# Issuing the stores of h and the attention transposes at group heads instead of at score bursts

## The chip, the cores and the metric

The kernel runs on one core of one Trainium2 chip. The metric is the device time of one execution in microseconds (us). Where the text says "shift", it compares two traces: how much earlier the same instruction starts, with the difference of the kernels' starts (up to 0.4 us, in one run 1.27 us) taken off, measured at the first residual add of the stage. Each trace is of one execution.

## The reference, cut to what matters

```python
def _A_ref(x, wqkv, wo):                 # 32 heads of 32, window of 256
    qkv = ...(x @ wqkv)...
    p = softmax(where(mask, q @ k.T * Dh ** -0.5, -1e9))
    return (p @ v) @ wo
def _B_ref(x, w1, w2):
    return silu(x @ w1) @ w2

h  = x + _A_ref(_layernorm(x), wqkv, wo)      # x: 2048 x 1024 bf16
h2 = h + _B_ref(_layernorm(h), w1, w2)        # w1: 1024 x 3584
```

## The kernel before

The work goes in four blocks of 512 rows. While TensorE (PE) does the dense matmuls of one block, it does the attention of another in bursts between them (a burst is a short row of score matmuls). The last such stage is 24 dense groups of the output projection (blocks 0 to 2) with the attention of block 3 in between. Each pair of groups completes one tile of 128 rows of h, which is stored to memory. Block 0 of h is read back within the same stage (`L497`), normalised, and transposed by DMA (`L203`) for the MLP that follows. VectorE (DVE) adds the residual to each half tile and does the norms. All these DMAs are issued by one sequencer, SP, in program order.

Two kinds of DMA are not issued where their data is made, but put on the list `late`: the store of a finished tile of h (`L276`) and the transpose of a head group's attention output (`L413`). `run_late` issues what is on the list.

```python
def run_late():
    while late:
        late.pop(0)()

def wo_group(b, j, c, between=None):
    acc = next_acc()                                   # one of two PSUM banks
    for g in range(G):
        if between: between(g)
        nc.tensor.matmul(acc, lhsT=qT[b][...], rhs=wo[...], ...)              # L271
    nc.vector.tensor_tensor(out=t_out[j % 2][...], in0=acc,
                            in1=r_in[(b * 4 + j) % 6][...], op=ALU.add)       # L273
    if c == 1:
        late.append(lambda: nc.sync.dma_start(out=h_dram[...], in_=t_out[j % 2]))  # L276

class Stream:                                          # ... cut
    def between(self, kt):
        if self.seen * 20 >= self.done * 192:
            run_late()                                 # at each burst of scores
            self.bursts[self.done]()
            self.done += 1
        ...                                            # cut: attention outputs

# the last stage; the stage of the dense groups before it is built alike
for n in range(24):
    if n % 2 == 0 and n >= 2 and n // 2 + 5 < S // P:
        load_res(n // 2 + 5)                           # residual load, L258
    wo_group(*dense[n], stream.between)
    if n in (1, 4, 7, 12, 15):
        load_w1((1, 4, 7, 12, 15).index(n))            # L518
    if n == 9:
        steps = ln2_steps(0); steps.pop(0)()           # reads block 0 of h, L497
    if n == 17:
        nc.sync.dma_start(out=w2[0], in_=w2_v[:, 0:4, :])                     # L595
    ...                                                # cut: steps of the layer norm
```

The softmax here doesn't subtract the row's maximum and nothing guards it: scores larger than these inputs give would overflow.

Of the kernel before, what the change touches and what calls it, by code (L numbers as in the profile page):

```python
# [48 lines left out]
def kernel(  # L49
# [89 lines left out]
    def load_x(b, j, queue=nc.sync):  # L139
        queue.dma_start(out=x_ring[(b % 2) * 4 + j], in_=x2d[(b * 4 + j) * P:(b * 4 + j + 1) * P, :])  # L140
# [94 lines left out]
    def v_group(b, j, c, copy, between=None):  # L235
        acc = next_acc()
        for kt in range(KT):
            if between:
                between(kt)
            nc.tensor.matmul(acc, lhsT=lnT_b[b % 2][:, kt, j * P:(j + 1) * P], rhs=wv[:, kt, c * 512:(c + 1) * 512],  # L240
                             start=(kt == 0), stop=(kt == KT - 1))
        copy(out=v[:, b * 4 + j, c * 16:(c + 1) * 16, 0:DH], in_=acc.rearrange("p (h d) -> p h d", d=DH))

    def qk_group(b, which, g, copy, between=None):
        acc = next_acc()
        col0 = which * D + g * P
        for kt in range(KT):
            if between:
                between(kt)
            nc.tensor.matmul(acc, lhsT=wqk[:, kt, col0:col0 + P], rhs=lnT_b[b % 2][:, kt, :],  # L250
                             start=(kt == 0), stop=(kt == KT - 1))
        copy(out=(qT, kT)[which][b][:, g, :], in_=acc)  # L252
# [4 lines left out]
    def load_res(t):  # L257
        nc.sync.dma_start(out=r_in[t % 6], in_=x2d[t * P:(t + 1) * P, :])  # L258
# [3 lines left out]
# [5 lines that stand above are left out]
        acc = next_acc()  # L267
        for g in range(G):
            if between:
                between(g)  # L270
            nc.tensor.matmul(acc, lhsT=qT[b][:, g, j * P:(j + 1) * P], rhs=wo[:, g, c * 512:(c + 1) * 512],  # L271
                             start=(g == 0), stop=(g == G - 1))
        nc.vector.tensor_tensor(out=t_out[j % 2][:, c * 512:(c + 1) * 512], in0=acc,  # L273
                                in1=r_in[(b * 4 + j) % 6][:, c * 512:(c + 1) * 512], op=ALU.add)
        if c == 1:
            late.append(lambda: nc.sync.dma_start(out=h_dram[(b * 4 + j) * P:(b * 4 + j + 1) * P, :], in_=t_out[j % 2]))  # L276
# [139 lines left out]
    def attn_piece(b, g, first, last):  # L416

        for k in range(2):
            a, z = max(first - 16 * k, 0), min(last - 16 * k, 16)
            if a < z:  # L420
                attn_out(b, g + k, a, z)
                if z == 16:
                    late.append(lambda k=k: attn_transpose(b, g + k))

    class Stream:
# [7 lines left out]

        def between(self, kt):
            if self.seen * 20 >= self.done * 192:
                run_late()
                self.bursts[self.done]()
                self.done += 1
            if self.seen * 40 >= (self.given * 2 + 1) * 192:
                if pending:  # L440
                    pending.pop(0)()
                coming.append(lambda b=self.b, n=self.given: attn_piece(b, n // 5 * 2, *SPLIT[n % 5]))
                if len(coming) > 2:
                    pending.append(coming.pop(0))
                self.given += 1
            self.seen += 1
# [38 lines left out]
    def ln1_steps(b):  # L485
        st, rs = ln_tiles("a")
        xs = [x_ring[(b % 2) * 4 + j] for j in range(4)]
        steps = [lambda j=j: ln_stats(xs[j], st, j) for j in range(4)]
        steps += rstd_steps(st, rs)
        for j in range(4):  # L490
            steps.append(lambda j=j: ln_norm(xs[j], st, rs, j))
        return steps, [lambda j=j: ln_transpose(xs[j], lnT_b[b % 2], j) for j in range(4)]

    def ln2_steps(b):
        st, rs = ln_tiles("b")
        hb = h_blk[b]
        load = lambda: nc.sync.dma_start(out=hb, in_=h_dram[b * 512:(b + 1) * 512, :].rearrange("(j p) d -> p j d", p=P))  # L497
        steps = [load]
        steps += [lambda j=j: ln_stats(hb[:, j, :], st, j) for j in range(4)]
        steps += rstd_steps(st, rs)  # L500
        for j in range(4):
            steps.append(lambda j=j: ln_norm(hb[:, j, :], st, rs, j))
        turns = [lambda j=j: ln_transpose(hb[:, j, :], ln2T[b], j) for j in range(4)]
        return steps[:-2] + [turns[0], steps[-2], turns[1], steps[-1]] + turns[2:]
# [12 lines left out]
    def load_w1(kt):  # L517
        nc.sync.dma_start(out=w1[:, kt, :], in_=w1_v[:, kt, :])  # L518
# [32 lines left out]
    for b in range(2, NB):  # L551
        stream = Stream(b - 1)
        dense = [lambda j=j, c=c: v_group(b, j, c, dve, stream.between) for j in range(4) for c in range(2)]
        dense += [lambda w=w, g=g: qk_group(b, w, g, dve, stream.between) for g in range(G) for w in range(2)]
        if b + 1 < NB:
            for j in range(4):
                load_x(b + 1, j)
            steps, turns = ln1_steps(b + 1)
        else:
            steps, turns = [], []  # L560
            nc.sync.dma_start(out=wo[:, 0:4, :], in_=wo_v[:, 0:4, :])
            nc.sync.dma_start(out=wo[:, 4:8, :], in_=wo_v[:, 4:8, :])
            load_res(0)
            load_res(1)
        for n in range(24):
            if b == NB - 1 and n in (4, 10, 14):
                load_w1({4: 7, 10: 6, 14: 5}[n])
            dense[n]()
            if steps and n >= 1 and n != 3:
                steps.pop(0)()  # L570
            elif turns and n % 3 == 2:
                turns.pop(0)()
        assert not steps and not turns
# [9 lines left out]
    steps = []  # L583
    stream = Stream(NB - 1)
    for n in range(24):
        if n % 2 == 0 and n >= 2 and n // 2 + 5 < S // P:
            load_res(n // 2 + 5)
        wo_group(*dense[n], stream.between)
# [3 lines that stand above are left out]
            steps = ln2_steps(0)  # L592
            steps.pop(0)()
        if n == 17:
            nc.sync.dma_start(out=w2[0], in_=w2_v[:, 0:4, :])  # L595
        for _ in range(1 if n < 16 else 2):
            if steps and n >= 12:
                steps.pop(0)()
# [105 lines left out]
```

## Time and profile before

| | before |
|---|---|
| time, first three runs | 696.37, 696.53, 699.1 us |
| span of the profiled run | 695.9 us |
| PE busy | 687.7 us |
| idle PE at tile 6's wait, at tile 10's wait, before the MLP | 0.39, 0.59, 1.97 us |
| read of block 0 of h (`L497`) issued | 254.16 us |
| last transpose of the MLP's input (`L203`) landed | 290.61 us |

A tile's number counts the tiles of 128 rows of h; tile t is made by groups 2t and 2t + 1. "Landed" is the time at which the DMA's completion semaphore is full, in the trace.

### The profile page before, as it was taken

What the parts mean: (1) busy time and instruction counts of PE and PEld (TensorE: products, weight loads), DVE (VectorE), ACT (ScalarE), POOL (GpSimd) and SP (SyncE); (2) the same over time, 40 slices, a digit from 0 to 9 for tenths busy, and PEclk for the clock granted to TensorE, in tenths of its full rate; (3) what the DMA queues carried; (4) which work ended last, traced back from release to release, by engine and by line L of the source; (5) the groups of instructions that cost most, each with busy time, mean ns of one, the idle gap of its engine ahead of it and who ended that gap; (6) DMA issues with size and microseconds to landing.
All of it is one profiled execution on the core that took longest, in us unless ns stands there. A gap on an engine that the chain in (4) does not pass through costs nothing.

```text
span 695.9 us, 13820 instructions
## 1 busy us (share of the span) xinstructions
PE 687.7 (99%) x5859; PEld 330.0 (47%) x5859; DVE 292.0 (42%) x616; ACT 240.7 (35%) x400; POOL 161.6 (23%) x295
## 2 busy tenths in 40 slices
PE   8999999999999999899999999999999999999998
PEld 3444455555555555444444444444444444444445
DVE  6267646744444438544315134433133251244111
ACT  4326656666666666421310023300033100233000
POOL 1007666666666656500000000000000000000000
PEclk9999999999999999999999999999999999999999
DMA  7732241236462988970023410023200023100110
GB/s 241 257 59 72 33 103 43 25 64 179 74 131 19 237 238 247 231 285 31 31 75 99 106 38 1 1 89 71 83 1 1 11 95 91 45 1 1 30 39 24
DMA packets 76462, 60.93 MB, mean 88 GB/s; under 512 B 50288, under 2 KB 60528, under 8 KB 76400
## 3 DMA queue, kind: packets, MB, share of 16 engines
q1 hardware_dynamic: 76256, 59.78, 32.7%
q8 instruction: 46, 0.75, 0.5%
q10 hardware_dynamic: 144, 0.26, 0.1%
q14 instruction: 16, 0.13, 0.1%
HBM read 39.85 MB, written 8.39 MB: 69 GB/s over the span
## 4 chain that ended last, share of the span: by engine, by line
PE 94%; DVE 2%; DMA 1%; issue 1%; POOL 1%; SPq 0%; ACT 0%; DVEq 0%; POOLq 0%
PE hacc L614 19%; PE hacc L651 17%; PE acc L250 16%; PE acc L651 10%; PE acc L614 9%; PE acc L240 8%; PE acc L271 4%; PE o_ps L377 3%; PE sc L302 2%; PE hacc L271 1%; PE o_ps L392 1%; DVE ln_st L171 1%; DMA h_dram<-r_t 1%; PE sc L348 1%; DVE r_t L273 1%
## 5 line engine op out<-in xcount | busy, mean ns | idle before, releaser
L368 POOL TENSOR_SCALAR_AFFINE_SELECT r_e<-r_e 128x512 bf16<-128x512 bf16 (+1 forms) x288 | 158.6, 568 | 127.6 <-ACT r_e L357 64.9
L651 PEld LDWEIGHTS <-r_a 128*128 128x128 bf16 x952 | 90.9, 98 | 103.0
L614 PEld LDWEIGHTS <-r_w 128*128 128x128 bf16 x896 | 87.4, 98 | 107.2 <-issue 2.4
L651 PE MATMUL hacc<-r_a 128*128 128x512 bf16 (+2 forms) x616 | 122.5, 360 | 0.0
L614 PE MATMUL hacc<-r_e,r_w 128*128 128x512 bf16 x456 | 100.9, 379 | 0.0
L314 ACT ACTIVATE r_e<-sc 128x768 bf16<-128x768 f32 x96 | 78.2, 814 | 49.9 <-PE sc L302 49.9
L623 ACT ACTIVATE r_n<-hacc 128x512 f32<-128x512 f32 x30 | 17.9, 597 | 178.9 <-PE hacc L614 178.9
L651 PE MATMUL acc<-r_a 128*128 128x512 bf16 x336 | 74.0, 379 | 0.0
L250 PEld LDWEIGHTS <-r_w 128*128 128x128 bf16 x512 | 44.9, 97 | 47.3 <-issue 0.2
L252 DVE CAST r_a<-acc 128x512 bf16<-128x512 f32 x56 | 38.6, 690 | 57.1 <-PE acc L250 57.1
L250 PE MATMUL acc<-r_t,r_w 128*128 128x512 bf16 x256 | 61.7, 379 | 0.0
L250 PE MATMUL acc<-r_w 128*128 128x512 bf16 x256 | 59.9, 379 | 0.0
L271 PE MATMUL acc<-r_o,r_a 128*128 128x512 bf16 x208 | 52.4, 379 | 1.1 <-DVE r_t L273 1.0
L614 PE MATMUL acc<-r_e,r_w 128*128 128x512 bf16 x216 | 49.1, 379 | 0.0
L377 PEld LDWEIGHTS <-r_e 128*128 128x128 bf16 x1152 | 37.8, 96 | 14.2
L357 ACT ACTIVATE r_e<-sc 128x1024 bf16<-128x1024 f32 x36 | 34.9, 1021 | 21.2 <-PE sc L348 20.1
L377 PE MATMUL o_ps<-r_a,r_e 128*128 128x33 bf16 x1152 | 38.3, 178 | 0.0
L666 DVE SCALAR_TENSOR_TENSOR r_t<-hacc,r_t 128x512 bf16<-128x512 f32 (+2 forms) x22 | 14.0, 635 | 57.0 <-PE hacc L651 57.0
L315 ACT ACTIVATE r_e<-sc 128x256 bf16<-128x256 f32 x96 | 37.6, 392 | 0.0
L666 DVE SCALAR_TENSOR_TENSOR r_t<-acc,r_t 128x512 bf16<-128x512 f32 x12 | 8.3, 691 | 64.2 <-PE acc L651 64.2
L624 DVE SCALAR_TENSOR_TENSOR r_a<-r_n,hacc 128x512 bf16<-128x512 f32 x30 | 20.6, 687 | 33.1 <-ACT r_n L623 33.1
L271 PEld LDWEIGHTS <-r_a 128*128 128x128 bf16 x256 | 21.8, 97 | 24.0 <-issue 2.1
(75 smaller groups left out, 539.5 us busy)
## 6 DMA issues: line engine op xcount, KB each, us to landing
r_w<-in_B_w_dram SPq DMA_DIRECT2D x8, 896.0 KB, 7.1
r_a<-in_B_w_dram SPq DMA_DIRECT2D x7, 1024.0 KB, 7.8
r_w<-in_A_wqkv_dram SPq DMA_DIRECT2D x6, 1024.0 KB, 8.7
h_dram<-r_t SPq DMA_DIRECT2D x16, 256.0 KB, 3.2
r_t<-h_dram SPq DMA_DIRECT2D x16, 256.0 KB, 2.8
out_dram<-r_t SPq DMA_DIRECT2D x31, 128.0 KB, 1.7
r_o<-in_A_x_dram SPq DMA_DIRECT2D x15, 256.0 KB, 3.9
r_e<-h_dram SPq DMA_DIRECT2D x3, 1024.0 KB, 5.6
```

What stands on the lines that cost most here:

```text
L240: nc.tensor.matmul(acc, lhsT=lnT_b[b % 2][:, kt, j * P:(j + 1) * P], rhs=wv[:, kt, c * 512:(c + 1) * 512], start=(kt == 0), stop=(kt == KT ...
L250: nc.tensor.matmul(acc, lhsT=wqk[:, kt, col0:col0 + P], rhs=lnT_b[b % 2][:, kt, :], start=(kt == 0), stop=(kt == KT - 1))
L252: copy(out=(qT, kT)[which][b][:, g, :], in_=acc)
L271: nc.tensor.matmul(acc, lhsT=qT[b][:, g, j * P:(j + 1) * P], rhs=wo[:, g, c * 512:(c + 1) * 512], start=(g == 0), stop=(g == G - 1))
L314: nc.scalar.activation(out=tri[:, :, :, 64:256], in_=both, func=ACT.Exp, scale=scale)
L315: nc.scalar.activation(out=e[:, 1024:1280].rearrange("p (h q) -> p h q", q=P), in_=bank[:, :, 192:320], func=ACT.Exp, scale=scale)
L357: nc.scalar.activation(out=e, in_=sc[pair], func=ACT.Exp, scale=scale)
L368: nc.gpsimd.affine_select(out=dst, in_=src, pattern=[[0, n] for n in dst.shape[1:-1]] + [[sgn, P]], compare_op=ALU.is_ge if upper else ALU ...
L377: nc.tensor.matmul(o_ps[pair][:, qt * 2 + hh, 0:VW], lhsT=chunk_of(i, bank, piece, pair, hh), rhs=v[:, b * 4 + kt, g * 4 + pair * 2 + hh, ...
L614: nc.tensor.matmul(acc, lhsT=w1[:, kt, ft * P:(ft + 1) * P], rhs=ln2T[b][:, kt, :], start=(kt == 0), stop=(kt == KT - 1))
L651: nc.tensor.matmul(acc[:, 0:c1 - c0], lhsT=gT[:, ft, j * P:(j + 1) * P], rhs=w2[ft // 4][:, ft % 4, c0:c1], start=(ft == 0), stop=(ft == F ...
L666: nc.vector.scalar_tensor_tensor(out=t_out[j % 2][:, c0:c1], in0=acc[:, 0:c1 - c0], scalar=0.5, in1=t_in[j % 2][:, c0:c1], op0=ALU.mult, o ...
```

## The change

The intent: issue the stores and the transposes at the head of each dense group, and not in the middle of one.

```diff
         def between(self, kt):
             if self.seen * 20 >= self.done * 192:
-                run_late()
                 self.bursts[self.done]()
                 self.done += 1
@@
         for n in range(24):
+            run_late()
             if b == NB - 1 and n in (4, 10, 14):
                 load_w1({4: 7, 10: 6, 14: 5}[n])
             dense[n]()
@@
     stream = Stream(NB - 1)
     for n in range(24):
+        run_late()
         if n % 2 == 0 and n >= 2 and n // 2 + 5 < S // P:
             load_res(n // 2 + 5)
         wo_group(*dense[n], stream.between)
```

## The prediction

> **What bounds the kernel now.** I began with the page: busy times, then the chain that ended last, then TensorE's (PE's) idle time.
>
> ```profile
> PE 687.7 (99%) x5859; PEld 330.0 (47%) x5859; DVE 292.0 (42%) x616; ACT 240.7 (35%) x400; POOL 161.6 (23%) x295
> PE 94%; DVE 2%; DMA 1%; issue 1%; POOL 1%; SPq 0%; ACT 0%; DVEq 0%; POOLq 0%
> ```
>
> PE is busy 687.7 of 695.9 us, so all its idle time is 8.2 us, and no reordering of transfers can give more: 8.2/695.9 = 1.2%, below 2%. Where is that idle time? The change touches the attention output transposes and the stores of h, so I tabulated engines by stretch over the output-projection stage, 227 to 291 us: the 24 groups of L271, the stores of L276, the residual loads of L258. Columns: stretch, length, busy PE, PEld, DVE, ACT, POOL, then PE clock, DMA share, GB/s.
>
> ```profile
> 227.00:254.00 27.00, 27.00 (x463) 14.28 (x454) 11.59 (x25) 18.33 (x32) 17.54 (x29) 1.00 0.93 231
> 254.00:289.00 35.00, 33.73 (x570) 17.75 (x569) 23.88 (x60) 22.46 (x40) 23.16 (x37) 1.00 0.94 242
> 289.00:291.00 2.00, 0.19 (x1) 0.13 (x2) 0.57 (x1) 0.00 (x0) 0.81 (x2) 1.00 0.95 257
> ```
>
> PE is full until 254, then loses 35.00 - 33.73 = 1.27 us, then 1.81 us: 3.08 us in all. In the stretch before 254 nothing can be won. The timeline of PE (start, length, what, and in brackets the idle time before) says where it is lost:
>
> ```profile
> 262.63 1.02 PE L271 MATMUL acc<-r_o,r_a 128*128 128x512 bf16 x4 [0.39 <-DVE r_t L273]
> 283.57 0.59 PE L271 MATMUL acc<-r_o,r_a 128*128 128x512 bf16 x2 [0.59 <-DVE r_t L273]
> 290.81 1.45 PE L614 MATMUL acc<-r_a,r_w 128*128 128x512 bf16 x6 [1.97 <-issue]
> ```
>
> The first two wait for a residual add (L273) that frees one of two accumulators. The third is the first matmul of the MLP. And the timeline of DVE for the adds that came late:
>
> ```profile
> 261.89 0.69 DVE L273 TENSOR_TENSOR r_t<-acc,r_a 128x512 bf16<-128x512 f32 x1 [4.11 <-PE o_ps L377]
> 277.31 0.69 DVE L273 TENSOR_TENSOR r_t<-acc,r_t 128x512 bf16<-128x512 f32 x1 [0.95 <-DMA h_dram<-r_t]
> 282.82 0.69 DVE L273 TENSOR_TENSOR r_t<-acc,r_a 128x512 bf16<-128x512 f32 x1 [1.98 <-PE sc L302]
> ```
>
> These are the first halves of row tiles 6, 9 and 10, with 2 output buffers: each must wait for the store of the tile two before. That store's issue and time to landing: tile 4, 255.14 + 6.7 = 261.8; tile 7, 271.50 + 5.7 = 277.2; tile 8, 277.00 + 5.7 = 282.7. All three agree with the adds' starts within 0.1 us, so the releaser named in the first and third lines is not the true one; it is the store. The SP queue around the end of the stage:
>
> ```profile
> 269.17 1.20 SPq L413 DMA_TRANSPOSE r_a<-r_n  x1
> 270.41 0.58 SPq L518 DMA_DIRECT2D r_w<-in_B_w_dram  x1
> 271.08 0.38 SPq L258 DMA_DIRECT2D r_a<-in_A_x_dram  x1
> 271.50 0.43 SPq L276 DMA_DIRECT2D h_dram<-r_t  x1
> 272.03 0.58 SPq L595 DMA_DIRECT2D r_a<-in_B_w_dram  x1
> ...
> 284.85 1.53 SPq L413 DMA_TRANSPOSE r_a<-r_n  x1
> 286.42 2.66 SPq L203 DMA_TRANSPOSE r_a<-r_a  x2
> 289.18 0.53 SPq L276 DMA_DIRECT2D h_dram<-r_t  x1
> ```
>
> L203 are the transposes of the MLP's first input. The last two sit behind an attention transpose (L413) that was held until DVE's norm at 284.78; they land 2.8 us after issue, the last one about 290.6, and PE starts at 290.8. The page calls this wait "issue"; the first weight load of the MLP waits in the program on the four L203, so I read it as the last of these.
>
> **What the Trainium skill says.** (1) "Perfetto Trace Analysis", section "DMA Instruction — HWDGE (DVE, Sync)": the reported window is only the sequencer's issue, the data movement is not in it, and the completing semaphore write comes after the write is confirmed, which can take surprisingly long when the target is HBM. The trace agrees: tile 4's store has an issue of 0.42 us and lands after 6.7 us. (2) "DMA: Bandwidth & Descriptors", section "Anatomy of one DMA": DMA engines do not wait on semaphores, the wait sits on the issuing sequencer. So one blocked entry holds all behind it on that queue. The trace agrees: SP issued nothing between 282.82 and 284.85 although the two L203 behind L413 were to come. (3) Same page, "Queues, rings and completion order": each DMA engine takes descriptors in ring order. The trace agrees in so far as small stores issued behind 1 MB loads land after 5.7 us, against 2.4 us at 289.18.
>
> **The change part by part.** I compared the two built programs' instruction order. PE, DVE, ACT and POOL: the same instructions in the same order, nothing added or removed (only some semaphore numbers differ). On SP the first 70 entries of 185 are identical, so everything before about 233 us, with three attention blocks' worth of transposes, does not change at all, although the diff touches that loop too. Entries 70 to 109 are permuted, all within the output-projection stage:
> - Each h store now stands ahead of the next residual load. Both wait for the same add, so the store goes out one load issue earlier: 0.33 to 0.43 us by the SP timeline, and ahead of 256 KB of data. The load goes later by the same, but is used ten groups later: free.
> - L413 is issued at a group head. It follows the 1 MB read of h (L497), where it went before it. Its results are read only in the MLP stage, and its source has three buffers: free, except for what stands behind it.
> - The w1 load that stood behind the L413 of 269.17 now stands before it. Its group ended near 267, so I expect it 3 to 4 us earlier. The DMA share was 0.18 in 268:269 and 0.00 in 269:270, so this fills a hole of some 2 us, and the store of tile 7 no longer queues behind that load's start.
> - The last two L203 now stand before the L413. The first is ready at once, at about 282.9; the second waits for its norm, which ended at 284.21. Issued at about 284.3, with 2.8 to 3.7 us to land, it is there at 287.1 to 288.0. PE's last group of the stage ends at 288.84.
>
> Sum on the path: the gap before the MLP falls from 1.97 to about 0: 1.97. The stall by tile 8's store: that store goes out about 1 us sooner (behind L413, ahead of a load) and has less in front; the 0.59 goes. A smaller slowness at 274.41 (five matmuls take 1.53 us and not 1.24, 0.29) belongs to the late add chain, and I count half, 0.15. Tile 6's stall of 0.39 stays: tile 4's store still stands behind L497, now with an L413 (1.20 us of issue) between, while L497 itself may go 0.4 to 0.7 us sooner, because tile 3's store does. I put 0.3 us of loss there. Sum: 1.97 + 0.59 + 0.15 - 0.3 = 2.4 us. 696.5 - 2.4 = 694.1 us, or 0.35%.
>
> **The rivals.**
> (a) *Nothing moves*: the DMA share is 0.94 in 254:289, so the same bytes might land at the same time in whatever order, and the MLP still starts at 290.8. For it: landing times of 5 to 6 us show a backlog. Against it: the share in 286:288 is 0.45 and 0.58, so the last two transposes waited for issue, not for the engines. Time then: 696.5.
> (b) *A new head-of-queue wait*: L413 now stands behind L497, which waits for tile 3's store, and it in turn holds tile 4's store. If it costs that store 1.5 us, tile 6's add and PE slip as much, the layer-norm work behind moves too, and with the other gains kept the sum is about -0.9: 695.6. If L413's own norm comes late near 276, it delays tile 8's store as well: up to 697.
> (c) *More than I count*: tile 6's stall goes too, and all 3.08 us of the stage: 693.4. Past that lie only idle stretches that the change does not reach.
>
> **Range and chances.** The most it can win is about 3.1 us (693.4); (a) and (b) reach 697. The three runs of before spread from 696.37 to 699.1, so I widen a little: 692.8 to 697.0. A gain over 2% would be 13.9 us, more than PE's whole idle time, so faster has 0.01. A loss over 2% would need 14 us of new stalls from 40 permuted entries: 0.01. Within 2%: 0.98.
>
> **What would show it right or wrong.** In the changed profile: PE busy still 687 to 688; all up to 230 us the same within 0.1; in the SP timeline the last two L203 before the L413, issued by about 285.7; the idle before the first L614 matmul under 0.4 us and its start at 288 to 289; the w1 load at 266 to 268 and the DMA hole at 269 filled; the 1.98 us DVE wait for tile 10 under 1; the one for tile 6 still 3.5 to 5. I am wrong if the first L614 matmul starts at 290 or later: then transfers, not their order, set it; or if a stall at tile 5 to 7 eats the gain.

## The result, and the profile after

The changed kernel takes 693.59 us (median of 4 runs, 693.36 to 693.7) against 697.74 us for the kernel before (4 runs, 696.37 to 699.1). The ratio is 0.994, 95% interval 0.9914 to 0.9966. A ratio is the mean time of one kernel's runs over the mean of the other's of the same rounds, so it is not quite the ratio of the medians quoted beside it. By the 2% rule this is "same", as predicted, but it is clear of noise. The span in the trace fell by 4.0 us, from 695.9 to 691.9.

In the changed kernel, lines from the removed one to the first added one are numbered one less, and lines behind the second one more: `L496` is the read of h, `L517` the w1 load, `L615` the first MLP matmul.

The page of the changed kernel, engines and chain:

```profile
PE 687.3 (99%) x5859; PEld 330.1 (48%) x5859; DVE 292.5 (42%) x616; ACT 240.8 (35%) x400; POOL 161.8 (23%) x295
PE 99%; DMA 0%; DVE 0%; issue 0%
```

PE has the same work. The chain that ends last is now PE for 99%, where 5% of it had been DVE, DMA, issue and POOL. The same three stretches as in the prediction:

```profile
227.00:254.00 27.00, 27.00 (x463) 14.29 (x459) 11.54 (x25) 18.33 (x32) 17.61 (x29) 1.00 0.96 245
254.00:289.00 35.00, 35.00 (x589) 18.88 (x590) 24.82 (x60) 22.55 (x41) 23.60 (x38) 1.00 1.05 252
289.00:291.00 2.00, 2.00 (x26) 1.05 (x23) 0.69 (x1) 0.51 (x1) 0.00 (x0) 1.00 0.76 167
```

All the idle time of PE in this stage is gone. DVE's timeline for the three adds that were late (first halves of tiles 6, 9 and 10):

```profile
259.58 0.69 DVE L273 TENSOR_TENSOR r_t<-acc,r_a 128x512 bf16<-128x512 f32 x1 [1.85 <-PE acc L271]
...
274.81 0.69 DVE L273 TENSOR_TENSOR r_t<-acc,r_t 128x512 bf16<-128x512 f32 x1
...
279.49 0.69 DVE L273 TENSOR_TENSOR r_t<-acc,r_a 128x512 bf16<-128x512 f32 x1 [0.82 <-PE acc L271]
```

They start 2.31, 2.50 and 3.33 us earlier than before. Where DVE still waits (the two brackets), it is for PE's own result. And PE's timeline where the stage ends:

```profile
286.12 1.02 PE L271 MATMUL acc<-r_o,r_a 128*128 128x512 bf16 x4
286.98 1.89 PE L615 MATMUL acc<-r_a,r_w 128*128 128x512 bf16 x8
```

The first MLP matmul starts at 286.98, not 290.81, and no bracket stands behind it: no wait. I laid the matmuls of the two traces side by side in order (5859 in each). The changed kernel is ahead by 0.05 us up to tile 6's wait, then gains 0.55 us at 262.6, 0.29 at 275.4, 0.81 at 283.6 and 2.13 at the MLP's start: 3.78 us in four steps. From there to the end nothing changes.

Why is this more than the idle time that the PE timeline shows (0.39 + 0.59 + 1.97)? A matmul of 512 columns stands in the trace with 0.379 us, but in an unbroken row one starts every 0.216 us (eight take 1.89 us in all: (1.89 - 0.379)/7). Records overlap, so each break in the row shows about 0.16 us less idle time than it costs: 0.39 + 0.16 = 0.55, 1.97 + 0.16 = 2.13; at 283.6 this rule gives 0.75, and the rest of the 0.81 was gained at 278. The 0.29 has no bracket in the timeline, but PE is busy 1.87 of the 2.00 us from 274 to 276: 0.13 us idle, and 0.13 + 0.16 = 0.29. The Trainium skill warns of this in kind ("Perfetto Trace Analysis", section "Tensor Engine Instruction (MATMUL, LD_WEIGHTS)"): a matmul's end is computed from its size and not observed.

The queue of SP in the changed kernel, in two places (with the read of h, and with the last transposes):

```profile
248.00 0.33 SPq L276 DMA_DIRECT2D h_dram<-r_t  x1
248.37 0.43 SPq L258 DMA_DIRECT2D r_t<-in_A_x_dram  x1
250.62 0.38 SPq L496 DMA_DIRECT2D r_a<-h_dram  x1
251.11 2.28 SPq L413 DMA_TRANSPOSE r_a<-r_n  x1
253.49 0.53 SPq L276 DMA_DIRECT2D h_dram<-r_t  x1
...
275.98 1.64 SPq L203 DMA_TRANSPOSE r_a<-r_a  x1
278.14 0.33 SPq L276 DMA_DIRECT2D h_dram<-r_t  x1
278.52 0.43 SPq L258 DMA_DIRECT2D r_t<-in_A_x_dram  x1
279.01 5.49 SPq L203 DMA_TRANSPOSE r_a<-r_a  x3
284.60 1.21 SPq L413 DMA_TRANSPOSE r_a<-r_n  x1
```

The last three transposes of the MLP's input go out in one row, and the attention transpose behind them. The last lands at 286.58, 0.40 us ahead of its use. In all ten traces that show a wait before the MLP, PE starts 0.20 us after the last of these landings, whatever releaser the trace names; so it is this landing that ends the wait, and 0.2 us of room are left here. The surprise is the read of h: issued at 250.62, not at 254.16. The queue of the kernel before, for that place:

```profile
248.04 0.33 SPq L258 DMA_DIRECT2D r_t<-in_A_x_dram  x1
248.42 0.43 SPq L276 DMA_DIRECT2D h_dram<-r_t  x1
250.72 1.20 SPq L413 DMA_TRANSPOSE r_a<-r_n  x1
254.16 0.38 SPq L497 DMA_DIRECT2D r_a<-h_dram  x1
254.63 0.46 SPq L258 DMA_DIRECT2D r_a<-in_A_x_dram  x1
255.14 0.42 SPq L276 DMA_DIRECT2D h_dram<-r_t  x1
```

The read of h has to wait until tile 3 is stored. Before, that store landed at 254.09; now at 250.57, although it was issued only 0.42 us earlier. While SP waited, it issued nothing else, and the DMA engines ran dry. Engines by stretch for 252 to 256 us, before and then after (the last two columns are the DMA share and GB/s):

```profile
252.00:256.00 4.00, 4.00 (x83) 2.43 (x82) 1.98 (x4) 2.84 (x7) 3.12 (x6) 1.00 0.59 59
```

```profile
252.00:256.00 4.00, 4.00 (x85) 2.44 (x84) 1.94 (x4) 2.84 (x7) 3.13 (x6) 1.00 1.00 278
```

### The profile page after: what moved, and what is told of

It reads as the page before. It is cut to its first block, busy times and chain, and to the rows that moved or that the text cites. A ratio compares the mean times of both kernels' runs of the same rounds, so it can differ in the third digit from the quotient of the medians.

```text
span 691.9 us, 13823 instructions
## 1 busy us (share of the span) xinstructions
PE 687.3 (99%) x5859; PEld 330.1 (48%) x5859; DVE 292.5 (42%) x616; ACT 240.8 (35%) x400; POOL 161.8 (23%) x295
## 4 chain that ended last, share of the span: by engine, by line
PE 99%; DMA 0%; DVE 0%; issue 0%
PE hacc L615 19%; PE hacc L652 17%; PE acc L250 16%; PE acc L652 10%; PE acc L615 9%; PE acc L240 8%; PE acc L271 7%; PE o_ps L377 4%; PE sc L302 3%; PE hacc L271 1%; PE o_ps L392 1%; PE sc L348 1%; PE sc L328 1%; DMA r_o<-in_A_x_dram 0%; PE tp L218 0%; DVE ln_st L171 0%
## 5 line engine op out<-in xcount | busy, mean ns | idle before, releaser
L652 PEld LDWEIGHTS <-r_a 128*128 128x128 bf16 x952 | 90.9, 98 | 103.0
L615 PEld LDWEIGHTS <-r_w 128*128 128x128 bf16 x896 | 87.5, 98 | 105.0
L615 PE MATMUL hacc<-r_e,r_w 128*128 128x512 bf16 x456 | 100.9, 379 | 0.0
L615 PE MATMUL acc<-r_e,r_w 128*128 128x512 bf16 x216 | 49.1, 379 | 0.0
L615 PE MATMUL hacc<-r_a,r_w 128*128 128x512 bf16 x144 | 32.9, 379 | 0.0
```

The lines of the kernel that those rows point to most:

```text
L615: nc.tensor.matmul(acc, lhsT=w1[:, kt, ft * P:(ft + 1) * P], rhs=ln2T[b][:, kt, :], start=(kt == 0), stop=(kt == KT - 1))
L652: nc.tensor.matmul(acc[:, 0:c1 - c0], lhsT=gT[:, ft, j * P:(j + 1) * P], rhs=w2[ft // 4][:, ft % 4, c0:c1], start=(ft == 0), stop=(ft == F ...
```

## The experiments

Twelve runs were made, two of them of the kernels before and after again; all gave correct results. The questions: is it the order on the queue or the amount of data that sets each landing; which half of the change does it; and are the named effects all there is?

**1. The last two transposes alone.** The kernel before; in group 21 nothing is flushed at the bursts, but at the head of group 22.

```diff
-                run_late()
+                if not hold[0]:            # hold[0] is set for n == 21
+                    run_late()
@@ last stage, head of the loop
+        if n == 22:
+            run_late()
```

> The kernel before with one reordering alone: in group 21 of the last attention stage nothing is flushed at the bursts, so the last two transposes of the MLP's input (L203) go ahead of the attention transpose that they stood behind. Theory A (order: PE waited 1.97 us at the MLP's start because these two were issued late): they are issued about 2 us sooner, the idle time before the first L614 matmul falls from 1.97 to between 0 and 0.8 us, the stalls of 0.39 and 0.59 us before it stay, and the kernel gains 1.3 to 2.1 us. Theory B (throughput: the DMA engines are busy anyway and data lands when it lands): the idle time stays at 1.5 us or more and the gain is under 0.5 us.

Measured: 695.67 us against 697.65 (ratio 0.9964, 0.9943 to 0.9985). PE's timeline in this run (its lines are renumbered: `L272` is the projection's matmul, `L620` the MLP's):

```profile
262.33 1.02 PE L272 MATMUL acc<-r_o,r_a 128*128 128x512 bf16 x4 [0.32 <-DVE r_t L274]
283.11 0.59 PE L272 MATMUL acc<-r_o,r_a 128*128 128x512 bf16 x2 [0.48 <-DVE r_t L274]
288.83 1.89 PE L620 MATMUL acc<-r_a,r_w 128*128 128x512 bf16 x8 [0.44 <-issue]
```

The earlier stalls stay, the wait before the MLP falls from 1.97 to 0.44 us, and the MLP starts 1.75 us earlier. Theory A is right for this part, in the presence of the other stalls. The last transpose was issued 3.1 us sooner (284.44 against 287.77, with 0.23 us of that the start), but landed only 1.8 us sooner (288.62 against 290.61, less the same 0.23). So it took 4.2 us from issue to landing and not 2.8, and a part of what the order gives is lost there.

**2 and 3. The two halves.** Run 2 takes the kernel before and issues only the stores at the group heads. Run 3 takes the changed kernel and issues only the transposes there, while the stores stay at the bursts. Both split the list by kind.

```diff
 # run 2                                        # run 3
 between:  run_late(("turn",))                  run_late(("store",))
 head:     run_late(("store",))                 run_late(("turn",))
```

> Half of the change: the stores of h are issued at the head of a group, ahead of the residual load, but the attention transposes at the bursts as before. Theory A: the stalls of L271 (0.39 and 0.59 us of idle PE, 1.65 us of shift together with the slow spot at 275) are the stores' doing and vanish or more than halve, gain 1.0 to 1.7 us; the MLP's start still waits, 1 to 2 us, because the last two L203 still stand behind the held attention transpose. Theory B: the stalls stay within 0.3 us of what they were. Theory C (the transposes of the attention output ahead of the w1 loads and the h read are what delays the stores): as B for the stalls, and the gain comes in the twin run instead.

> The other half: attention transposes are issued at the head of a group and the stores of h at the bursts, behind the residual load, as before. Theory A: the MLP's start no longer waits (idle under 0.5 us, gain about 2 us), while the stalls of L271 at tiles 6, 9 and 10 stay for the most part (0.5 to 1.6 us of shift). Theory C: the stalls vanish here too and the gain is that of the whole change, 3.8 us in the trace. Theory B: no more than 0.5 us gained.

Measured: run 2 took 694.78 us (ratio 0.9961, 0.9941 to 0.9981), run 3 694.49 us (0.9963, 0.9935 to 0.999; one of its six runs took 699.27, at a granted clock of 0.995). In run 2 the stalls of the stage vanish and the MLP still waits, 1.26 us, as theory A has it. In run 3 the MLP does not wait, but theory A missed the rest: 0.55 and 0.81 us were gained at tiles 6 and 10 as well, though every store stands behind the residual load. The MLP starts 3.48 us earlier with the transposes alone, 2.36 with the stores alone, 3.78 with both. The halves overlap. Theory C is out too: it wanted the stalls to stay in run 2. What both have in common with the whole change is an early read of h: 251.86 and 251.56 us.

**4. The changed kernel with the attention transpose held in front of the last two again.**

```diff
         def between(self, kt):
             if self.seen * 20 >= self.done * 192:
+                if hold[0]:                # hold[0] is set for n == 21
+                    run_late()
                 self.bursts[self.done]()
```

> The changed kernel with one step undone: in group 21 the attention transpose is flushed at the burst again, so the last two L203 stand behind it and behind DVE's norm. Theory A: the MLP's start waits again, 1 to 2.1 us of idle PE before the first L614 matmul, the rest of the gain (1.7 us) stays, so the kernel is 1 to 2.1 us slower than the changed one. Theory B: under 0.4 us slower, as in the changed kernel the last L203 lands only 0.4 us ahead of need and the engines are busy.

Measured: 694.54 us (ratio 0.9952, 0.9931 to 0.9973). PE's timeline:

```profile
289.60 1.89 PE L620 MATMUL acc<-r_a,r_w 128*128 128x512 bf16 x8 [2.03 <-issue]
```

In this trace the wait is back in full, and the gains at tiles 6 to 10 stay (1.65 us of shift): 2.19 us of shift undone (3.78 - 1.59). But it was taken of the slowest of six executions: it took 696.23 us, the other five 694.06 to 694.76. By the clock, the changed kernel run later on took 693.93 us, so 0.6 us less and not the 1 to 2.1 us expected; the two were not in the same rounds. Together with run 1 this shows that the place of this one transpose brings a wait before the MLP; how much it costs in most executions is not shown.

**5. The waits for stores taken away by another means.** The kernel before with its order, but three output buffers for the tiles.

```diff
+    t_out3 = [*t_out, view(r_a, 32768, 1024)]
@@ wo_group
-        nc.vector.tensor_tensor(out=t_out[j % 2][...], in0=acc,
+        to = t_out[j % 2] if b == NB - 1 else t_out3[(b * 4 + j) % 3]
+        nc.vector.tensor_tensor(out=to[...], in0=acc,
                                                # cut: the store, which reads to
```

> The kernel before with the queue's order untouched, but three output buffers of h for the twelve tiles of the stage and not two, so that no residual add has to wait for the store of two tiles before. Theory A1 (PE's stalls at 262.6, 275.4 and 283.6 us are the adds' wait for a store and nothing else): these stalls vanish, 1.65 us by the trace, and the wait at the MLP's start stays, 1.5 to 2.2 us of idle PE. Rival A2 (the adds are late for another reason, DVE's own load or the residual's load): under 0.5 us of shift before the MLP.

Measured: 695.39 us against 697.89 (ratio 0.9973, 0.9954 to 0.9993). The shift before the MLP is 1.65 us, the number expected to the hundredth: A1 is shown. The releasers that the trace named for two of these waits (PE) were wrong, as the prediction read them. The wait before the MLP fell to 1.17 us, lower than expected: DVE, no longer held up, had the norms ready sooner, and the held transpose went out at 281.73.

**6. What tile 3's store queued behind.** The kernel before with one w1 load moved from before that store to behind it.

```diff
-        if n in (1, 4, 7, 12, 15):
-            load_w1((1, 4, 7, 12, 15).index(n))
+        if n in (1, 4, 8, 12, 15):
+            load_w1((1, 4, 8, 12, 15).index(n))
```

> The kernel before with one load moved: the 896 KB of w1 that is issued after group 7, in front of the store of tile 3, is issued after group 8, behind that store. It tests why tile 3's store landed at 254.1 us before and at 250.6 to 251.7 in three reordered versions. Theory W (the store queues behind this load, whose last piece comes late): the store lands within 3.5 us of its issue at 248.4, so by 252, and the read of h is issued by 252.3 and not at 254.2. Rival X (the w1 load has no part in it; the time is the store's own): the store still lands 5 us or more after its issue. For the time of the kernel I expect within 1 us of before, as the load then stands in front of the read of h.

Measured: 697.0 us (ratio 0.9987, 0.9966 to 1.0009). The queue of SP:

```profile
248.66 0.43 SPq L276 DMA_DIRECT2D h_dram<-r_t  x1
249.14 0.42 SPq L518 DMA_DIRECT2D r_w<-in_B_w_dram  x1
...
252.34 0.46 SPq L497 DMA_DIRECT2D r_a<-h_dram  x1
```

The store landed at 251.70, 3.04 us after issue and not 5.67, and the read of h was issued at 252.34. Theory W holds: in the kernel before, the store waited behind the w1 load. It does not say why the store lands sooner in the changed kernel, where this load still stands in front (244.94); no run isolates that. In the trace tile 6's stall is gone, the wait before the MLP stays (1.91 us), and the MLP starts 1.16 us earlier than before. The clock shows no gain. One reason is in the trace, which is of the slowest of four executions (698.12 us, mean granted clock 0.997): right behind the wait, the granted clock (the column before the DMA share) halves.

```profile
290.00:293.50 3.50, 3.50 (x22) 1.47 (x21) 0.00 (x0) 0.18 (x1) 0.00 (x0) 0.51 0.74 182
```

The MLP's first eight matmuls take 3.40 us here and not 1.89. The traces of the kernel before, of run 4 and of run 11 have waits of 1.97 to 2.03 us there and a clock of 1.00 behind them, so that the wait brings it about is not shown.

**7. Both effects by other means.** Run 5's third buffer and run 1's order of the last two, nothing else.

> Neither half of the change as such, but both of its effects by other means: three output buffers, and the last two transposes of the MLP's input ahead of the attention transpose (as in the first experiment). If the account is full (1.65 us of waits for stores and 1.75 to 2.1 us at the MLP's start), no PE stall is left in the stage (all under 0.3 us), the first L614 matmul starts 3.3 to 3.9 us earlier than before, and the time is that of the changed kernel within 0.6 us. If the change did something else besides, this kernel stays 1 us or more behind it.

Measured: 694.7 us (ratio 0.9955, 0.9939 to 0.9972). A miss: by the clock it stays 0.77 us behind the changed kernel of the same rounds (run 8), where at most 0.6 was expected, and in the trace:

```profile
288.13 1.89 PE L622 MATMUL acc<-r_a,r_w 128*128 128x512 bf16 x8 [1.18 <-DVE r_a L276]
```

The stage's stalls are gone, but PE waits 1.18 us before the MLP although the last three transposes now go out in one row. The last lands at 287.93, and PE starts 0.20 us later; DVE, named as releaser, had ended its add before that transpose landed (last add 286.99 + 0.69 = 287.68). The shift is 2.44 us, 1.34 short of the changed kernel. So the order of those last two matters (runs 1 and 4) but is not enough.

**8. The changed kernel again.**

> The changed kernel again, on the same chip as the three others, for the comparison and for a second trace: no PE stall over 0.1 us between 227 and 291 us, the last transpose of the MLP's input landing before 287.3, time 3.3 to 4.6 us under before.

Measured: 693.93 us (693.73 to 694.03) against 697.89 (ratio 0.9943, 0.9928 to 0.9958). The shift is 3.78 us once more, the last transpose landed at 286.66. This trace lacks 111 matmul records, and shows eight gaps of 0.16 us between groups for it; no other idle time in the stage.

**9 and 10. Is it the last w1 load?** In the changed kernel it is issued at 263.92 and not at 270.41, ahead of the stretch from 268 to 270 us in which the DMA engines had been nearly idle (shares 0.18 and 0.00). Run 9 undoes that (the flush at the bursts of group 15), run 10 adds it to run 7.

```diff
 # run 9, on the changed kernel; run 10, on run 7
-        hold[0] = n == 21                      -        hold[0] = n == 21
+        hold[0] = n == 15                      +        hold[0] = n in (15, 21)
```

> The changed kernel with another step undone: after group 15 the attention transpose is flushed at the burst, so the last w1 load (896 KB) stands behind it again, and behind DVE's norm that it waits for. The run with both other effects left 1.18 us of idle PE at the MLP's start. Theory W (the last load, 4 us earlier, fills an idle stretch of the DMA engines near 269 us, and the last transposes land earlier for it): that load is issued at about 267.5 and not at 263.9, the last L203 lands near 288.1 and not 286.6, PE waits 0.8 to 1.4 us at the MLP's start, and no other stall returns; 0.8 to 1.4 us slower than the changed kernel. Rival V (the place of the load does not matter; the two other effects were short of the whole for some other reason, such as where the stores stand): idle under 0.3 us and the time of the changed kernel.

> The run with both effects by other means, and as a third the last w1 load ahead of the attention transpose after group 15. Theory W: now the account is full: the last L203 lands by 287.0, the idle time at the MLP's start falls from 1.18 to under 0.3 us, the first L614 matmul starts 3.5 to 4.0 us earlier than before (corrected for the start), and the time is that of the changed kernel within 0.6 us. Rival V: 1 us or more of idle time stays.

Measured: run 9 took 694.0 us (ratio 0.9946, 0.9933 to 0.9959), with the load at 268.44, no wait before the MLP and a shift of 3.75 us. Theory W falls: in the changed kernel the load's place is worth nothing. Run 10 took 694.23 us (0.9948, 0.9934 to 0.9962), and its trace still has 0.64 us of idle PE before the MLP, with a shift of 2.97 us. That lies between the two theories (under 0.3, 1 or more). The trace is of its slowest execution (695.74 us, the other four 693.69 to 694.35), with a start late by 1.27 us, so I don't lean on the 0.53 us of shift that it has over run 7.

**11. The kernel before again.**

> The kernel before, for a second trace. If its stalls are of the program and not of one execution: idle PE of 0.3 to 0.6 us near 262.6 and near 283.6 and of 1.7 to 2.2 us before the first L614 matmul, within 0.3 us of those times.

Measured: 697.82 us (ratio 1.0002, 0.998 to 1.0023). The waits at 283.2 (0.76 us) and before the MLP (2.02 us) are there. The one at tile 6 has no bracket, but its five matmuls take 1.53 us and not 1.24: it is there with 0.29 us, about half of the 0.55 before. Run 1, which has the same order up to there, shows it with 0.32 us of idle time. So the stall varies from execution to execution.

**12. The queue's blocked head.** Run 7 with the list split by kind as in run 2, and at the head of group 18 the attention transpose ahead of the residual load.

```diff
+        if n == 18:
+            run_late(("turn",))
```

> The run with both effects by other means (it left 1.18 us of idle PE at the MLP's start), plus one thing: at the head of group 18 the attention transpose that is due is issued ahead of the residual load, not behind it. The residual load waits for the add of tile 8, so all behind it waits too: the attention transpose (1.20 us of issue), the store, and the first transpose of the MLP's input, which went out at 277.0 us although its norm had ended near 276.2. Theory Q (the blocked load at the head of the queue is the third part of the change): the attention transpose is issued near 273.3 and not 274.6, the first L203 about 1 us sooner, the last L203 lands near 287.0 and the idle time falls from 1.18 to 0.4 us or less; time that of the changed kernel within 0.6 us. Rival (transfers set it): 0.8 us or more stays.

Measured: 694.54 us against 696.88 (ratio 0.9963, 0.9946 to 0.9979). The queue of SP:

```profile
273.60 1.21 SPq L422 DMA_TRANSPOSE r_a<-r_n  x1
...
276.28 2.92 SPq L204 DMA_TRANSPOSE r_a<-r_a  x1
...
280.35 5.74 SPq L204 DMA_TRANSPOSE r_a<-r_a  x3
```

The first half came as expected: the attention transpose at 273.60, the first transpose of the MLP's input 1.2 us sooner than in run 7 (276.28 against 276.99, with 0.52 us between the starts). But that one's issue took 2.92 us and not 2.11 as in run 7 (1.64 in the changed kernel), most of the gain was lost there, and 0.83 us of idle time stayed. Theory Q explains a third at most, 0.35 us of shift; the rival (0.8 us or more stays) is nearer.

What divides the kernels that wait from those that do not? Two columns do:

| kernel | last two before the attention transpose | read of h issued | GB/s in 252:256 | idle PE before the MLP | shift at the MLP |
|---|---|---|---|---|---|
| before | no | 254.16 | 59 | 1.97 | 0 |
| before again (11) | no | 253.95 | 60 | 2.02 | 0.30 |
| last two alone (1) | yes | 254.07 | 43 | 0.44 | 1.75 |
| third buffer (5) | no | 254.00 | 51 | 1.17 | 2.45 |
| both by other means (7) | yes | 254.43 | 44 | 1.18 | 2.44 |
| with group 18 (12) | yes | 254.59 | 64 | 0.83 | 2.79 |
| stores alone (2) | no | 251.86 | 115 | 1.26 | 2.36 |
| changed, one undone (4) | no | 251.28 | 237 | 2.03 | 1.59 |
| transposes alone (3) | yes | 251.56 | 230 | none | 3.48 |
| changed, w1 held (9) | yes | 250.53 | 280 | none | 3.75 |
| changed, and again (8) | yes | 250.62, 250.99 | 278, 270 | none | 3.78, 3.78 |

(Runs 6 and 10 are left out: run 6 has a w1 load in front of the read, run 10 a start that is 1.27 us late. The times of issue and the stretch are not corrected for the start.) Only kernels with both have no wait. One reading is a debt of transfers: with the read of h about 3.5 us later, about 4 us x 220 GB/s = 0.9 MB (an estimate from the two lines above, 278 - 59 GB/s) move behind 256 us, and the last transposes land about 1.3 us later for it. The traces speak against so plain a chain. In the kernel before, the DMA engines were empty again long before the last transposes:

```profile
269.00:270.00 1.00, 1.00 (x29) 0.43 (x27) 1.00 (x3) 0.04 (x1) 0.93 (x3) 1.00 0.00 0
```

Run 1 has the same 0 GB/s there, and in runs 7 and 12 the DMA share from 268 to 271 us is 0.52 and 0.69. So little of what was put off at 254 us can have been left at 271. What the traces show is nearer to the end. The issue of the first transpose of the MLP's input ends at 279.10 in run 7 and 279.20 in run 12, but at 277.62 to 278.35 in the four traces with the right order and no wait (the changed kernel twice, runs 3 and 9). The last three start at 280.25 and 280.35, not at 279.01 to 279.52, and take 5.71 and 5.74 us of issue, not 5.07 to 5.51. Why they do is open: no run moved the read of h alone on top of run 7. So the second column is an association in eleven traces, and about 1.3 us of the 3.78 (what run 7 lacks) has no shown cause.

## Why the prediction was right or wrong

- *The range*: right. 693.59 us lies in 692.8 to 697.0 and the change is within 2%. That it is only 0.5 us from the 694.1 of the sum is luck: the base was 1.24 us too low (696.5 for 697.74) and the gain 1.75 us too small (2.4 for 4.15).
- *The change does nothing before 230 us*: right. The same matmuls start within 0.05 us up to tile 6's wait.
- *The wait before the MLP, 1.97 us, goes to 0*: right in size (2.13 in shift) and right that the held attention transpose brings a wait (runs 1 and 4). Short in mechanism: it assumed an issue at about 284.3 and 2.8 to 3.7 us to landing; the last one was issued at 281.87 and took 4.7, and the MLP started at 286.98, not at 288 to 289. Run 7 shows that with this order a wait of 1.18 us can be left, even when no add waits for a store.
- *Tile 8's store, 0.59*: right; 0.81 in shift. *The slow spot at 274.41, half of 0.29*: the whole 0.29. Run 5 shows that both, with tile 6's, are the adds' wait for stores.
- *Tile 6's stall stays, with 0.3 us of loss*: wrong, and it is the largest error. PE gained 0.55 us there, and DVE's wait was 1.85 us and not 3.5 to 5. The failing step is "`L497` itself may go 0.4 to 0.7 us sooner": it went 3.54 us sooner. The prediction moved the read by as much as the store in front of it was issued earlier. But the store's time from issue to landing was not a constant to be added: it fell from 5.67 to 2.57 us. (Run 6 shows that what stands in front sets it: 3.04 us with the w1 load behind.) The term thus was mis-sized by 0.85 us (from -0.3 to +0.55) and makes most of the gap between 2.4 us predicted and 3.78 measured. The other 0.5 is what the idle times shown at the MLP and at tile 10 understated (0.16 and 0.22 us) and the other half of the 0.29.
- *"The most it can win is about 3.1 us"*: wrong as a bound. The idle time of PE in a trace understates what a wait costs.
- *The w1 load fills the hole near 269 us*: it did go out early, at 263.92 (266 to 268 expected), and it is worth nothing (run 9).
- *Rival (a), transfers set the landing*: it lost here, as the MLP started 3.78 us earlier with the same bytes; in runs 7 and 12 something of the kind may remain. *Rival (b)*: the attention transpose behind the read of h did take 2.28 us of issue and not 1.20, and cost nothing, as the store behind it still left at 253.49, earlier than 255.14. *Rival (c), tile 6's stall goes too*: this is what happened, and its 693.4 us is the nearest of all.
- *The base*: 696.5 us was low. Over the later rounds the kernel before had medians of 697.65, 697.89, 697.84 and 696.88 us, with single runs from 695.7 to 700.0. The changed kernel's ten runs lie between 693.36 and 694.03. The spread shrank too. Part of it goes with the granted clock: of the 42 runs of before in those rounds, 12 have a mean of 0.997 or 0.998, among them all nine from 698.9 us up, while the ten of the changed kernel all have 1.000; at 0.999 or 1.000 the kernel before still reaches from 695.74 to 698.71. So a part of the 4 us by the clock is such executions. Run 6's trace shows one: half the clock for 3.4 us behind the wait before the MLP. That the waits bring them about is not shown.

## What to carry to other kernels

On an in-order DMA queue, look for the entry that waits at its head: everything behind it pays, and here the DMA engines ran dry meanwhile (59 GB/s against 278). Do not add a constant time to landing: it depends on what stands in front of the entry, and here a shift of 0.4 us in issue came with a landing 3.5 us sooner. Before blaming a late transfer on an earlier jam, look whether the engines ran empty in between. When PE is 99% busy, count what a wait costs by laying the matmuls of two traces side by side, not by the idle time shown; and see which of a kernel's executions a trace was taken of.

## What the Trainium skill lacked or had wrong

- "Perfetto Trace Analysis", section "Tensor Engine Instruction (MATMUL, LD_WEIGHTS)", says that a matmul's end is estimated, but not what follows: with records of 0.379 us at a spacing of 0.216 us, each wait shows about 0.16 us too little idle time (0.39 for 0.55, 1.97 for 2.13, 0.13 for 0.29).
- "DMA: Bandwidth & Descriptors", section "Issuing engines are not separate DMA queues", calls the sequencer's time to initiate a DMA usually small relative to the DMA itself. For the DMA transposes here, which that sentence does not except, it is not: 1.20 us of issue for one that lands after 2.3 us (269.17 in the kernel before), and three in a row took 5.49 us of issue in the changed kernel; in run 12 a single one took 2.92 us.
- "Runtime: NRT & Kernel Launch", section "Instruction fetch mechanics", says that instructions are refilled in 16 KiB blocks and that the cost is mostly hidden. In the DMA packets of the changed kernel's trace such a 16,384-byte packet comes every 6 to 12 us in this stage and takes 0.9 to 1.5 us on its engine, and soon after it some packets of a transpose (256 bytes, 0.018 us in the median) take far longer, up to 1.9 us at 282.9. That the one causes the other is not shown. What it costs was not measured.
